# Gate input x^T from plain float32 products in 32x64 array tiles, without block-diagonal halves and stacking DMAs

## The chip, the cores and the metric

The kernel runs on one core of a Trainium2 chip. The metric is the device time of one execution in microseconds (us); less is better. Engines are named as in the profile: PE is the matrix engine, PEld its weight loads, DVE the vector engine, ACT the scalar engine, POOL the general engine, SP the queue that issues the DMAs.

## What is computed

For each of 8 batches, 8 heads, 576 positions and a head width of 64, two attentions run one after the other, then a gated layer, then a spatial gated layer:

```python
p_packed = sm_attn(p, k, v)            # 32 packed queries per head
x = sm_attn(q, p_packed, p_packed)     # 576 x 512 per batch
gate = sigmoid(causal 5-tap convolution of x along the positions, per channel)
y = gate * (x @ w_val) @ w_out
h = relu(y @ w_in); u, v = halves of h
v_n = layer norm of v over its 512 channels
out = (u * (w_spatial @ v_n + b)) @ w_out2
```

The change concerns x, in its transposed form (channels on partitions), that the convolution reads. The product x @ w_val takes another way in both versions (below) and doesn't need x itself.

## The kernel before

Setup turns the weights from float64 words into float32 (`from_f64`: units on ACT, DVE and POOL), multiplies w_out and w_in into one matrix on PE (`fold`), and splits most matrices into a high and a low part in the type float32r. A product of two split matrices is then three float32r products (`mm3`); a plain float32 product needs no split.

The work of one batch is cut into steps with names, and three strings set the order in which they are written: START (setup and the attention of batch 0), FIRST (the rest of batch 0 with the attention of batch 1, mixed with setup) and LOOP (the rest of batch b with the attention of batch b+1). A scheduler then moves instructions within each engine's queue; all queues run strictly in order, and PSUM is a pool `ps2` of four slots of two banks each, so a step that needs a slot waits until the step that had it was copied out. The steps around the change:

- `sa`, `tr`, `av`: scores of p and k, exponentials, product with v. At its end `av` holds in PSUM, for a group g of four heads, 32 rows for each head: the packed values, and their sums in column 64. DVE makes the reciprocal `rs`, ACT writes the scaled values to `pp` (L203). DVE also writes `ppd`, the same values as block-diagonal halves: four multiplications by a 0/1 mask for each group (L199), split into `ppdh` and `ppdl` by `split` (L92 on ACT, L93 on DVE).
- `ppt`, `sb`: `pp` is transposed by PE (L212), copied by ACT (L214), and multiplied with q in plain float32 (L220): 16 products of 64 rows by 32 columns of the array, eight tiles side by side.
- `sb2`: softmax over the 32 packed positions. DVE ends it with `an` (L251), which is split into `Ah` and `Al` for the product with M. Four DMAs for each group (L259, L260) put the halves of `Ah` above those of `Al` in one tile `ad`.
- `m`: M = p_packed @ w_val in plain float32 (L269), eight products of 64x32 tiles and 512 columns, split into `Mh` (ACT) and `Ml` (DVE). x @ w_val is then A @ M, in `val`.
- `xt(g)`: x^T of two heads at a time, so that the channels fill 128 partitions: `ad` times `ppdh`, then `ppdl`, as full 128x128 products in float32r. Two channel tiles c for each g, four products each, 16 for a batch. `conv(c)` follows: ACT copies PSUM to `x` (L288) and writes `acc` with the last tap (L292), DVE adds four taps (L304; in batch 0 some go to POOL), ACT makes the sigmoid `gate` (L308).
- `sp`: the spatial product, 28 products for each of four tiles; DVE multiplies by u out of PSUM (L418), ACT and DVE split the result `g` (L92, L93).
- `out`: the last product, 24 for each of four tiles; `val` of the next round multiplies its result by `gate` on DVE (L331).

Of the kernel before, what the change touches and what calls it, by code (L numbers as in the profile page):

```python
# [18 lines left out]
ADB = 2  # L19
# [3 lines left out]
ik0 ip0 ro0 ic0 ik1 sa0 iv1 uo0 iv0 rw0 tr0 lv0 rv0 ro1 uo1 cw0 rv1 lk0 lq0 rw1 uw0 tr1 uo3 uw1 av0 uw2 uo2 uv0 av1 uv1 uw3 lq1 fv3 fv0 fv1 lk1 ppt0 sb0 sb20 sb21 fv2 xt0 uv3 uv2 lp0 m0 xt1 lv1  # L23
"""
FIRST = """
val1 ru1 val0 val3 ru0 lv0 val2 sa0 uu2 uu0 hv0 uu1 tr0 ws3 tr1 uu3 fu2 fu0 ws4 hv3 wo0 lv1 ws1 hv2 av0 av1 fu1 lq0 fu3 ppt0 lq1 wo1 hv1 hv4 ws0 sb0 hu1 hu2 ws2 sb20 lp0 hu3 sb21 hu0 wo3 lk0 lk1 sp0 sp2 sp1 wo2 sp3 xt0 m0 out1 out3 xt1 out0 out2
"""
LOOP = """
lq0 val1 val0 val2 lp0 val3 hu1 sa0 lq1 hv0 tr0 hv1 hu0 hv4 av0 tr1 av1 hu2 hv2 ppt0 hv3 sb0 sb20 sp1 lv0 sb21 hu3 sp0 sp3 sp2 m0 lk1 xt0 out1 lv1 xt1 out2 out0 lk0 out3
"""  # L30


# [1 line left out]
def packed_attention_gated_mlp(  # L34
# [36 lines left out]
    g_p = ctx.enter_context(tc.tile_pool(name="g", bufs=4))  # L71
    vr_p = ctx.enter_context(tc.tile_pool(name="vr", bufs=2))
    vn_p = ctx.enter_context(tc.tile_pool(name="vn", bufs=1))
    ad_p = ctx.enter_context(tc.tile_pool(name="ad", bufs=ADB))
    ug_p = ctx.enter_context(tc.tile_pool(name="ug", bufs=UGB))
    ps2 = ctx.enter_context(tc.tile_pool(name="ps2", bufs=4, space=bass.MemoryType.PSUM))

# [4 lines left out]
    mask = const.tile([P, 2, 64], F32)  # L82
# [40 lines left out]
    class Attn:  # L123
        def __init__(self, b):
            self.b = b
            self.a, self.aT, self.ppd = {}, {}, {}
            self.sT, self.A = {}, {}
            self.gate, self.ad = {}, {}

        def heads(self, lhsT, kind):  # L130
            src = [kq_t.pop((kind, self.b, i)) for i in range(2)]
# [45 lines left out]
        def av(self, g):  # L177
            aT = self.aT.pop(g)
            v = v_t.pop((self.b, g))
            ps = ps2.tile([P, 2, 512], F32, tag="ps2", name="ps2")[:, 0, :]  # L180
            for t in range(5):
                for h in range(4):
                    nc.tensor.matmul(  # L183
                        ps[NPK * h:NPK * h + NPK, :65],
                        lhsT=aT[:, 9 * (h // 2) + 4 * (h % 2) + t, :],
                        rhs=v[:, h, t, :],
                        start=(t == 0), stop=(t == 4),
                        tile_position=(0, NPK * h),
                    )
# [88 lines left out]
        def xt(self, g):
            ad = self.ad.pop(g)
            for i in range(2):  # L280
                ps = ps2.tile([P, 2, 512], F32, tag="ps2", name="ps2")
                for n in range(2):
# [362 lines left out]
```

## Time and profile before

| what | value |
|---|---|
| median of 3 runs | 643.06 us (642.97 to 643.32) |
| span of the profiled execution, first to last instruction | 642.7 us |
| PE busy | 593.3 us, 92% |
| DVE, ACT, POOL busy | 494.3, 314.7, 88.1 us |
| chain that ended last | PE 83%, DVE 9%, DMA 4%, ACT 2%, issue 2% |
| granted PE clock | mostly full; half in some stretches before 120 us |

No other time of the profiled execution is given than its span; the median lies 0.36 us above it. In the slices of 16 us each the digits are busy shares in tenths; a digit 9 for PE says that it was occupied, not that it ran at its peak, since its products are pipelined and their ends modelled. DMA queue 1 moved 61 MB in 28.8% of the time of its 16 engines.

### The profile page before, as it was taken

The numbers are of one execution on the slowest core, as the hardware profiler recorded it, in microseconds if no ns is written. First come the engines' busy times: TensorE is split into PE (matmuls) and PEld (weight loads), VectorE is DVE, ScalarE is ACT, GpSimd is POOL, SyncE is SP. The second block draws the span as 40 slices with busy tenths as digits, with TensorE's granted clock in tenths as the row PEclk, the third lists the DMA queues.
The fourth block names the chain that finished last, engine by engine and source line by source line (L and its number), as shares of the span: only waits on it lengthen the run. The fifth ranks groups of instructions, "written<-read, shape, count | busy, mean of one in ns | idle before, by whom it ended". The sixth has DMA issues, their size and how long they took to land.

```text
span 642.7 us, 12335 instructions
## 1 busy us (share of the span) xinstructions
PE 593.3 (92%) x5000; PEld 520.1 (81%) x5000; DVE 494.3 (77%) x966; ACT 314.7 (49%) x548; POOL 88.1 (14%) x92
## 2 busy tenths in 40 slices
PE   1466769899999999999999999999999999999997
PEld 0222535699988998899889998899889988999997
DVE  4989988986868877788679876887688867993630
ACT  2635755555554464437443635455444644372412
POOL 2396642221001000100010000100010001000100
PEclk9978789899999999999999999999999999999999
DMA  8961143341133312341323233231243110310001
GB/s 323 409 224 44 31 144 139 108 125 56 58 91 145 74 74 79 120 114 56 97 84 108 59 100 118 76 93 56 74 159 74 75 38 1 75 56 19 1 1 73
DMA packets 21689, 61.91 MB, mean 96 GB/s; under 512 B 2977, under 2 KB 4001, under 8 KB 21634
## 3 DMA queue, kind: packets, MB, share of 16 engines
q1 hardware_dynamic: 21634, 61.14, 28.8%
q8 instruction: 39, 0.64, 0.4%
q14 instruction: 16, 0.13, 0.1%
HBM read 42.25 MB, written 9.44 MB: 80 GB/s over the span
## 4 chain that ended last, share of the span: by engine, by line
PE 83%; DVE 9%; DMA 4%; ACT 2%; issue 2%; SPq 0%; POOL 0%; ACTq 0%; DVEq 0%; POOLq 0%
PE ps L97 77%; DMA stage<-wsT 2%; PE ps L143 2%; DVE acc L304 2%; PE ps L220 2%; PE ps L183 1%; DMA raw<-w_outT 1%; PE ps L269 1%; DVE tmp L460 1%; DVE tmp L464 1%; DVE tmp L459 1%; DVE ppd L199 1%; DMA raw<-w_out 1%; DVE sT L247 0%; DVE sm L245 0%
## 5 line engine op out<-in xcount | busy, mean ns | idle before, releaser
L97 PE MATMUL ps<-ws,vn 128*128 128x288 f32 (+1 forms) x896 | 124.0, 296 | 0.0
L97 PEld LDWEIGHTS ps<-ws,vn 128*128 128x128 f32 (+1 forms) x896 | 120.3, 188 | 2.9 <-issue 2.8
L97 PE MATMUL ps<-g,wp 128*128 128x288 f32 x768 | 114.2, 298 | 0.0
L97 PEld LDWEIGHTS ps<-g,wp 128*128 128x128 f32 x768 | 106.3, 188 | 5.0 <-DVE g L331 1.3
L97 PE MATMUL ps<-g,wo 128*128 128x288 f32 x768 | 104.3, 295 | 0.0
L97 PEld LDWEIGHTS ps<-g,wo 128*128 128x128 f32 x768 | 102.6, 188 | 0.8 <-ACT acc L292 0.8
L97 PE MATMUL ps<-wp,g 128*128 128x512 f32 x384 | 100.1, 411 | 2.9 <-DVE g L331 2.9
L304 DVE SCALAR_TENSOR_TENSOR acc<-x,cw,acc 128x572 f32<-128x572 f32 (+3 forms) x122 | 96.3, 854 | 3.3 <-ACT acc L292 2.8
L97 PEld LDWEIGHTS ps<-wp,g 128*128 128x128 f32 x384 | 72.1, 192 | 22.4 <-issue 3.5
L370 POOL TENSOR_TENSOR rstd<-rstd,mhalf 128x1 f32<-128x1 f32 (+1 forms) x40 | 22.9, 574 | 458.7 <-DVE rstd L369 456.4
L92 ACT CAST g<-g 128x576 fp32r<-128x576 f32 x64 | 43.1, 674 | 85.9 <-DVE g L418 55.0
L93 DVE TENSOR_TENSOR g<-g,g 128x576 fp32r<-128x576 f32 x64 | 48.1, 752 | 9.3 <-ACT g L92 8.9
L397 ACT ACTIVATE u<-ps 128x576 f32<-128x576 f32 x32 | 20.7, 647 | 47.1 <-PE ps L97 47.1
L92 ACT CAST vn<-vr 128x512 fp32r<-128x512 f32 (+1 forms) x40 | 24.7, 619 | 36.2 <-DVE vr L371 36.1
L418 DVE TENSOR_TENSOR g<-ps,u 128x576 f32<-128x576 f32 x32 | 24.1, 754 | 21.0 <-PE ps L97 20.9
L97 PE MATMUL ps<-Ah,Ml 128*128 128x288 f32 x128 | 38.6, 303 | 1.8 <-DVE Ml L93 1.8
L331 DVE TENSOR_TENSOR g<-ps,gate 128x576 f32<-128x576 f32 x32 | 24.1, 756 | 20.1 <-ACT gate L308 13.7
L97 PE MATMUL ps<-Ah,Mh 128*128 128x288 f32 x128 | 38.6, 301 | 0.7 <-ACT acc L292 0.7
L97 PE MATMUL ps<-Al,Mh 128*128 128x288 f32 x128 | 38.5, 301 | 0.0
L365 DVE BATCH_NORM_STATS2 st<-vr 128x6 f32<-128x512 f32 (+1 forms) x40 | 27.3, 683 | 11.8 <-ACT vr L358 10.2
L371 DVE TENSOR_SCALAR vr<-vr,mv,rstd 128x512 f32<-128x512 f32 (+1 forms) x40 | 22.5, 562 | 17.0 <-POOL rstd L370 16.7
L93 DVE TENSOR_TENSOR vn<-vr,vn 128x512 fp32r<-128x512 f32 (+1 forms) x40 | 27.1, 680 | 6.9 <-ACT vn L92 6.8
(115 smaller groups left out, 861.6 us busy)
## 6 DMA issues: line engine op xcount, KB each, us to landing
v<-vT SPq DMA_DIRECT2D x16, 650.0 KB, 5.4
kq<-kT SPq DMA_DIRECT2D x16, 576.0 KB, 4.6
kq<-qT SPq DMA_DIRECT2D x16, 576.0 KB, 4.7
outT<-o SPq DMA_DIRECT2D x32, 288.0 KB, 2.1
ad<-Ah SPq DMA_DIRECT2D x32, 144.0 KB, 2.5
ad<-Al SPq DMA_DIRECT2D x32, 144.0 KB, 2.5
raw<-w_in SPq DMA_DIRECT2D x8, 512.0 KB, 10.2
raw<-w_outT SPq DMA_DIRECT2D x4, 512.0 KB, 8.6
```

What stands on the lines that cost most here:

```text
L92: nc.scalar.copy(out=hi, in_=src)
L93: nc.vector.tensor_tensor(out=lo, in0=src, in1=f32(hi), op=ALU.subtract)
L97: nc.tensor.matmul(out, lhsT=a, rhs=b, start=(i == 0), stop=(i == len(pairs) - 1))
L143: nc.tensor.matmul(ps[g][NPK * qt:NPK * qt + NPK, h // 2, SQ * (h % 2):SQ * (h % 2) + SQ], lhsT=pT_, rhs=k[:, SQ * qt:SQ * qt + SQ], start ...
L220: nc.tensor.matmul(ps[g][NPK * h:NPK * h + NPK, n, :SH], lhsT=pT_, rhs=q[:, n * SH:(n + 1) * SH], start=True, stop=True, tile_position=(64 ...
L304: nc.vector.scalar_tensor_tensor(out=acc[:, sft:], in0=x[:, :S - sft], scalar=cw[:, c, tap:tap + 1], in1=acc[:, sft:], op0=ALU.mult, op1=A ...
L331: nc.vector.tensor_tensor(out=halves(t), in0=ps[:, :, :SH], in1=halves(at.gate.pop(c)), op=ALU.mult)
L365: nc.vector.bn_stats(st[:w], vr[:w])
L370: nc.gpsimd.tensor_tensor(out=rstd[:w], in0=rstd[:w], in1=mhalf[:w], op=ALU.pow)
L371: nc.vector.tensor_scalar(out=vr[:w], in0=vr[:w], scalar1=mv[:w, 0:1], scalar2=rstd[:w], op0=ALU.subtract, op1=ALU.mult,)
L397: nc.scalar.activation(out=halves(u), in_=ps[:, :, :SH], func=AF.Relu)
L418: nc.vector.tensor_tensor(out=halves(t), in0=ps[:, :, :SH], in1=halves(self.u.pop(c)), op=ALU.mult)
```

## The change

x^T is made from `pp` and `an` as they are. Each head is one plain float32 product of 32 rows (its packed positions) by 64 columns (its channels), at array row 32h and column 64g; the heads h and h+4 (g = 0 and 1) lie one above the other in a channel tile. `xt(n)` now makes all four channel tiles for one half n of the positions: 8 products into two PSUM slots, and ACT copies each slot to a half of `x` (a tile with two channel tiles in it). The four convolutions start when both halves are there, and ACT takes the last tap from `x` in SBUF instead of PSUM. `ppd`, its split, the mask and the DMAs to `ad` are gone. The channel order of w_val, conv_w and w_out follows the new pairs, on the host. `an` and `x` get pools of their own. In the strings xt0 and xt1 stand together, in LOOP ahead of m0.

```diff
-lq0 val1 val0 val2 lp0 val3 hu1 sa0 lq1 hv0 tr0 hv1 hu0 hv4 av0 tr1 av1 hu2 hv2 ppt0 hv3 sb0 sb20 sp1 lv0 sb21 hu3 sp0 sp3 sp2 m0 lk1 xt0 out1 lv1 xt1 out2 out0 lk0 out3
+lq0 val1 val0 val2 lp0 val3 hu1 sa0 lq1 hv0 tr0 hv1 hu0 hv4 av0 tr1 av1 hu2 hv2 ppt0 hv3 sb0 sb20 sp1 lv0 sb21 hu3 sp0 sp3 sp2 xt0 xt1 m0 lk1 out1 lv1 out2 out0 lk0 out3
...
-    ad_p = ctx.enter_context(tc.tile_pool(name="ad", bufs=ADB))
+    an_p = ctx.enter_context(tc.tile_pool(name="an", bufs=3))
+    x_p = ctx.enter_context(tc.tile_pool(name="x", bufs=2))
...
-            ppd = pp_p.tile([P, 2, 2, 64], F32, tag="ppd", name="ppd", bufs=1)
-            for i in range(2):
-                r = slice(64 * i, 64 * i + 64)
-                for j in range(2):
-                    nc.vector.scalar_tensor_tensor(
-                        out=ppd[64 * j:64 * j + 64, i], in0=ps[r, :64].unsqueeze(1).to_broadcast([64, 2, 64]),
-                        scalar=rs[r], in1=mask[r], op0=ALU.mult, op1=ALU.mult,
-                    )
             nc.scalar.activation(out=self.pp[:, g, :], in_=ps[:, :64], func=AF.Copy, scale=rs)
...
-            split(hi, lo, ppd)
...
-                nc.sync.dma_start(out=f32(ad)[:64, i], in_=f32(hi)[r])
-                nc.sync.dma_start(out=f32(ad)[64:, i], in_=f32(lo)[r])
...
-                    mms(ps[:, n, :SH], [(w[:, i, :], ad[:, i, n * SH:(n + 1) * SH]) for w in self.ppd[g]])
-                self.conv(2 * g + i, ps)
...
+        def xt(self, n):
+            ss = slice(n * SH, (n + 1) * SH)
+            ps = [ps2.tile([P, 2, 512], F32, tag="ps2", name="ps2") for _ in range(2)]
+            for h in range(4):
+                hs = slice(NPK * h, NPK * h + NPK)
+                for g in range(2):
+                    nc.tensor.matmul(
+                        ps[h // 2][64 * g:64 * g + 64, h % 2, :SH], lhsT=self.pp[hs, g, :],
+                        rhs=self.an[g][hs, ss], start=True, stop=True, tile_position=(NPK * h, 64 * g),
+                    )
+            if n == 0:
+                self.x = [x_p.tile([P, 2, S], F32, tag="x", name="x") for _ in range(2)]
+            for j in range(2):
+                nc.scalar.copy(out=self.x[j][:, :, ss], in_=ps[j][:, :, :SH])
+            if n == 1:
+                for c in range(4):
+                    self.conv(c, self.x[c // 2][:, c % 2, :])
...
-            nc.scalar.activation(
-                out=halves(acc), in_=ps[:, :, :SH], func=AF.Copy, scale=cw[:, c, CONV - 1:CONV]
-            )
+            nc.scalar.activation(out=acc, in_=x, func=AF.Copy, scale=cw[:, c, CONV - 1:CONV])
```

What stands where, in three places. First PE, in a round of LOOP, between the last `sp` product and the first `out`. Names are those of PSUM tiles; a row in square brackets waits for the engine named (the suffix is the same everywhere). Before:

```order
L97 MATMUL ps_3883<-ws_779,vn_739 128x288
L269 MATMUL ps_3917<-wval,ppT 32x512 [waits DVE_49]
L269 MATMUL ps_3917<-wval,ppT 32x512 x7
L97 MATMUL ps_3932<-ad,ppdh 128x288 [waits DMAHW3_49,DMAHW1_49,DVE_49]
L97 MATMUL ps_3932<-ad,ppdl 128x288
L97 MATMUL ps_3932<-ad,ppdh 128x288
L97 MATMUL ps_3932<-ad,ppdl 128x288
L97 MATMUL ps_3947<-ad,ppdh 128x288 [waits DMAHW4_49,DMAHW2_49,DVE_49]
```

Now:

```order
L96 MATMUL ps_3732<-ws_746,vn_706 128x288
L265 MATMUL ps_3766<-an,pp 64x288 [waits DVE_49] x2
L265 MATMUL ps_3766<-an,pp 64x288 x2
L265 MATMUL ps_3767<-an,pp 64x288 [waits DVE_49]
L265 MATMUL ps_3767<-an,pp 64x288 x3
L265 MATMUL ps_3780<-an,pp 64x288 [waits DVE_49]
L265 MATMUL ps_3780<-an,pp 64x288 x3
L265 MATMUL ps_3781<-an,pp 64x288 [waits DVE_49]
L265 MATMUL ps_3781<-an,pp 64x288 x3
L250 MATMUL ps_3824<-wval,ppT 32x512 [waits Activation_49]
L250 MATMUL ps_3824<-wval,ppT 32x512 x7
L96 MATMUL ps_3839<-g,wo_811 128x288 [waits Activation_49]
```

Before, `m` came first and waited for DVE alone, two of the four x^T tiles followed, and the other two stood behind the first `out` tile. Now all 16 x^T products come first, in four PSUM slots, and `m`, which needs one of these four again, waits for ACT. Second, ACT in the same round. Before:

```order
L92 CAST g<-g_3912 128x576
L92 CAST Mh<-ps_3917 128x1024
L288 COPY x<-ps_3932 128x576
L292 ACTIVATE acc<-ps_3932,cw 128x576
L288 COPY x<-ps_3947 128x576
L292 ACTIVATE acc<-ps_3947,cw 128x576
L441 COPY o<-ps_3962 128x576
```

Now:

```order
L91 CAST g<-g_3761 128x576
L272 COPY x<-ps_3766 128x2x288
L272 COPY x<-ps_3767 128x2x288
L272 COPY x<-ps_3780 128x2x288
L281 ACTIVATE acc<-x,cw 128x576 x2
L272 COPY x<-ps_3781 128x2x288
L281 ACTIVATE acc<-x,cw 128x576 x2
L91 CAST Mh<-ps_3824 128x1024
```

The first row of each is the high part of the last `sp` tile's result; behind it `Mh` moved from the first place to the last, and the x copies moved ahead. Third, DVE at the end of `av` in START. Before:

```order
L199 SCALAR_TENSOR_TENSOR ppd<-ps_263,rs,mask 64x128 x4
L460 SCALAR_TENSOR_TENSOR tmp<-raw,tmp 128x512
L193 TENSOR_SCALAR rs<-ps_322 128x1
L464 TENSOR_SCALAR tmp<-tmp 128x512
L93 TENSOR_TENSOR ppdl<-ppd,ppdh 128x256
L194 RECIPROCAL rs<-rs 128x1
L199 SCALAR_TENSOR_TENSOR ppd<-ps_322,rs,mask 64x128 x3
```

Now:

```order
L447 SCALAR_TENSOR_TENSOR tmp<-raw,tmp 128x512
L192 TENSOR_SCALAR rs<-ps_310 128x1
L451 TENSOR_SCALAR tmp<-tmp 128x512
L193 RECIPROCAL rs<-rs 128x1
L454 TENSOR_TENSOR winv<-winv,tmp 128x512
```

The ten `ppd` instructions of the batch are gone, and the setup units (`tmp`, `winv`) close up; the other setup units and the steps of `sb` stand on DVE in nearly the order of before.

## Rows read from the trace of the kernel before

**Rows 1.** Page, parts 1 and 2: busy us by engine; busy tenths in 40 slices.
```profile
PE 593.3 (92%) x5000; PEld 520.1 (81%) x5000; DVE 494.3 (77%) x966; ACT 314.7 (49%) x548; POOL 88.1 (14%) x92
...
PE   1466769899999999999999999999999999999997
...
DVE  4989988986868877788679876887688867993630
```

**Rows 2.** Chain that ended last, from 340 us: start, length (us), what.
```profile
357.17 1.02 PE ps L269 x16
358.19 21.55 PE ps L97 x161
```

**Rows 3.** The same chain, whole execution: the product `sb` and what follows.
```profile
337.77 1.13 PE ps L220 x32
338.90 18.27 PE ps L97 x136
```

**Rows 4.** Timeline, 356.3 to 361.5 us, all engines: start, length, instruction, [idle before].
```profile
357.10 1.09 PE L269 MATMUL ps<-wval,ppT 64*32 64x512 f32 x16
357.21 0.76 DVE L418 TENSOR_TENSOR g<-ps,u 128x576 f32<-128x576 f32 x1 [1.46 <-PE ps L97]
358.00 0.67 ACT L92 CAST g<-g 128x576 fp32r<-128x576 f32 x1 [3.04 <-DVE g L418]
...
358.12 0.40 PE L97 MATMUL ps<-ad,ppdh 128*128 128x288 f32 x1
...
358.36 0.29 PE L97 MATMUL ps<-ad,ppdl 128*128 128x288 f32 x1
...
358.58 1.01 ACT L92 CAST Mh<-ps 128x1024 fp32r<-128x1024 f32 x1
...
359.29 2.41 PE L97 MATMUL ps<-g,wo 128*128 128x288 f32 x17
359.48 0.64 ACT L288 COPY x<-ps 128x576 f32<-128x576 f32 x1
...
360.01 0.75 ACT L292 ACTIVATE acc<-ps,cw 128x576 f32<-128x576 f32 x1
```

**Rows 5.** Timeline of DVE, 348 to 388 us: the convolution's steps of one round.
```profile
360.80 11.85 DVE L304 SCALAR_TENSOR_TENSOR acc<-x,cw,acc 128x572 f32<-128x572 f32 x16
```

**Rows 6.** Waits of PE, whole execution: us in total, times, longest.
```profile
PE ps L220 <- DVE sT L232: 1.0, 1, 1.0
```

**Rows 7.** Timeline of DVE, 20 to 126 us.
```profile
24.10 1.44 DVE L199 SCALAR_TENSOR_TENSOR ppd<-ps,rs,mask 64x128 f32<-64x128 f32 x4
...
32.22 0.42 DVE L93 TENSOR_TENSOR ppdl<-ppd,ppdh 128x256 fp32r<-128x256 f32 x1
...
37.48 0.85 DVE L232 STREAM_TRANSPOSE sT<-ps 128x288 f32<-128x288 f32 x2 [1.96 <-PE ps L220]
...
61.24 0.76 DVE L251 STREAM_TRANSPOSE an<-sT 128x576 f32<-128x576 f32 x1
...
64.96 2.95 DVE L304 SCALAR_TENSOR_TENSOR acc<-x,cw,acc 128x572 f32<-128x572 f32 x2
...
113.99 1.44 DVE L199 SCALAR_TENSOR_TENSOR ppd<-ps,rs,mask 64x128 f32<-64x128 f32 x4
```

**Rows 8.** Timeline of PE, 0 to 130 us, and steady round (chain, from 130 us).
```profile
115.83 0.33 PE L212 MATMUL ps<-ident,pp 128*128 128x128 f32 x1 [2.13 <-ACT pp L203]
...
122.30 1.23 PE L220 MATMUL ps<-kq,ppT 64*32 64x288 f32 x32
...
197.79 2.80 PE ps L97 x12
```

**Rows 9.** Windows: us, PE busy (x), PEld, DVE, ACT, POOL, PEclk, DMA share, GB/s.
```profile
93.60:95.30 1.70, 0.21 (x2) 0.11 (x1) 0.29 (x2) 1.69 (x7) 1.38 (x2) 1.00 0.07 26
113.60:116.00 2.40, 0.27 (x3) 0.17 (x2) 2.31 (x6) 0.54 (x2) 2.32 (x2) 1.00 0.67 213
116.00:120.00 4.00, 4.00 (x13) 3.11 (x13) 3.99 (x8) 3.59 (x9) 0.45 (x1) 0.61 0.01 5
```

More of the change, by code (lines that the diff above doesn't have):

```diff
@@ L18 @@
 UGB = 5
-ADB = 2
 DADD = ('u2', 'o0', 'o1', 'w1', 'w0')
@@ L22 @@
 START = """
-ik0 ip0 ro0 ic0 ik1 sa0 iv1 uo0 iv0 rw0 tr0 lv0 rv0 ro1 uo1 cw0 rv1 lk0 lq0 rw1 uw0 tr1 uo3 uw1 av0 uw2 uo2 uv0 av1 uv1 uw3 lq1 fv3 fv0 fv1 lk1 ppt0 sb0 sb20 sb21 fv2 xt0 uv3 uv2 lp0 m0 xt1 lv1
+ik0 ip0 ro0 ic0 ik1 sa0 iv1 uo0 iv0 rw0 tr0 lv0 rv0 ro1 uo1 cw0 rv1 lk0 lq0 rw1 uw0 tr1 uo3 uw1 av0 uw2 uo2 uv0 av1 uv1 uw3 lq1 fv3 fv0 fv1 lk1 ppt0 sb0 sb20 sb21 fv2 xt0 xt1 uv3 uv2 lp0 m0 lv1
 """
 FIRST = """
-val1 ru1 val0 val3 ru0 lv0 val2 sa0 uu2 uu0 hv0 uu1 tr0 ws3 tr1 uu3 fu2 fu0 ws4 hv3 wo0 lv1 ws1 hv2 av0 av1 fu1 lq0 fu3 ppt0 lq1 wo1 hv1 hv4 ws0 sb0 hu1 hu2 ws2 sb20 lp0 hu3 sb21 hu0 wo3 lk0 lk1 sp0 sp2 sp1 wo2 sp3 xt0 m0 out1 out3 xt1 out0 out2
+val1 ru1 val0 val3 ru0 lv0 val2 sa0 uu2 uu0 hv0 uu1 tr0 ws3 tr1 uu3 fu2 fu0 ws4 hv3 wo0 lv1 ws1 hv2 av0 av1 fu1 lq0 fu3 ppt0 lq1 wo1 hv1 hv4 ws0 sb0 hu1 hu2 ws2 sb20 lp0 hu3 sb21 hu0 wo3 lk0 lk1 sp0 sp2 sp1 wo2 sp3 xt0 xt1 m0 out1 out3 out0 out2
 """
 LOOP = """
-lq0 val1 val0 val2 lp0 val3 hu1 sa0 lq1 hv0 tr0 hv1 hu0 hv4 av0 tr1 av1 hu2 hv2 ppt0 hv3 sb0 sb20 sp1 lv0 sb21 hu3 sp0 sp3 sp2 m0 lk1 xt0 out1 lv1 xt1 out2 out0 lk0 out3
+lq0 val1 val0 val2 lp0 val3 hu1 sa0 lq1 hv0 tr0 hv1 hu0 hv4 av0 tr1 av1 hu2 hv2 ppt0 hv3 sb0 sb20 sp1 lv0 sb21 hu3 sp0 sp3 sp2 xt0 xt1 m0 lk1 out1 lv1 out2 out0 lk0 out3
 """
@@ L81, in packed_attention_gated_mlp @@
     cw = const.tile([P, NC, CONV], F32)
-    mask = const.tile([P, 2, 64], F32)
     ident = const.tile([P, P], F32)
@@ L125, in __init__ @@
             self.b = b
-            self.a, self.aT, self.ppd = {}, {}, {}
-            self.sT, self.A = {}, {}
-            self.gate, self.ad = {}, {}
+            self.a, self.aT = {}, {}
+            self.sT, self.A, self.an = {}, {}, {}
+            self.gate = {}
         def heads(self, lhsT, kind):
@@ L194, in av @@
             nc.vector.reciprocal(rs, rs)
-            ppd = pp_p.tile([P, 2, 2, 64], F32, tag="ppd", name="ppd", bufs=1)
-            for i in range(2):
-                r = slice(64 * i, 64 * i + 64)
-                for j in range(2):
-                    nc.vector.scalar_tensor_tensor(
-                        out=ppd[64 * j:64 * j + 64, i], in0=ps[r, :64].unsqueeze(1).to_broadcast([64, 2, 64]),
-                        scalar=rs[r], in1=mask[r], op0=ALU.mult, op1=ALU.mult,
-                    )
-            nc.scalar.activation(out=self.pp[:, g, :], in_=ps[:, :64], func=AF.Copy, scale=rs)
-            ppd = ppd.rearrange("p a b c -> p a (b c)")
-            hi = pp_p.tile([P, 2, P], F32R, tag="ppdh", name="ppdh")
-            lo = pp_p.tile([P, 2, P], F32R, tag="ppdl", name="ppdl")
-            split(hi, lo, ppd)
-            self.ppd[g] = (hi, lo)
+            nc.scalar.activation(out=self.pp[:, g, :], in_=ps[:, :64], func=AF.Copy, scale=rs)
         def ppt(self, _):
@@ L249, in sb2 @@
             )
-            an = f_p.tile([P, S], F32, tag="f", name="an")
+            an = an_p.tile([P, S], F32, tag="an", name="an")
             nc.vector.transpose(out=an, in_=sT.rearrange("p a b -> p (a b)"))
@@ L255, in sb2 @@
             self.A[g] = (hi, lo)
-            ad = ad_p.tile([P, 2, S], F32R, tag="ad", name="ad")
-            for i in range(2):
-                r = slice(64 * i, 64 * i + 64)
-                nc.sync.dma_start(out=f32(ad)[:64, i], in_=f32(hi)[r])
-                nc.sync.dma_start(out=f32(ad)[64:, i], in_=f32(lo)[r])
-            self.ad[g] = ad
+            self.an[g] = an
         def m(self, _):
@@ L276, in m, with conv @@
             self.M = (hi, lo)
[L278 to L282, printed above, removed]
-                    mms(ps[:, n, :SH], [(w[:, i, :], ad[:, i, n * SH:(n + 1) * SH]) for w in self.ppd[g]])
-                self.conv(2 * g + i, ps)
-        def conv(self, c, ps):
-            x = f_p.tile([P, S], F32, tag="f", name="x")
-            nc.scalar.copy(out=halves(x), in_=ps[:, :, :SH])
+        def xt(self, n):
[15 more added lines that the diff above has]
+                    self.conv(c, self.x[c // 2][:, c % 2, :])
+        def conv(self, c, x):
             gt = ug_p.tile([P, S], F32, tag="ug", name="gate")
@@ L571, in packed_attention_gated_mlp @@
     nc.vector.memset(mhalf, -0.5)
-    nc.vector.memset(mask, 0.0)
-    for h in range(4):
-        nc.vector.memset(mask[32 * h:32 * h + 32, h % 2, :], 1.0)
     t = const.tile([P, NC, DM], F32, tag="ws0", name="woT")
@@ L613, in rows, with by_pair @@
         return np.ascontiguousarray(w.reshape(-1, 128, w.shape[1]).transpose(1, 0, 2))
-    w_val = np.asarray(inputs["moe_w_val"]).reshape(2, 4, D, -1)
+    def by_pair(w, axis):
+        w = np.moveaxis(np.asarray(w), axis, 0)
+        w = w.reshape(2, 4, D, -1).transpose(1, 0, 2, 3).reshape(H * D, -1)
+        return np.moveaxis(w, 0, axis)
     wt, bias = inputs["moe2_w_spatial"].T, inputs["moe2_b_spatial"]
@@ L626 @@
         "pT": pt,
-        "w_val": rows(w_val.transpose(1, 0, 2, 3).reshape(H * D, -1)),
-        "conv_w": rows(np.ascontiguousarray(inputs["moe_conv_w"].T)).reshape(128, -1),
-        "w_outT": rows(np.ascontiguousarray(inputs["moe_w_out"].T)),
+        "w_val": rows(by_pair(by_pair(inputs["moe_w_val"], 0), 1)),
+        "conv_w": rows(by_pair(inputs["moe_conv_w"].T, 0)).reshape(128, -1),
+        "w_outT": rows(by_pair(inputs["moe_w_out"], 0).T),
         "w_in": rows(inputs["moe2_w_in"]),
```

## Prediction

> **What bounds the kernel now.** I read the page first: PE is occupied 92% of the span, and from the eighth slice on its digit is 9 throughout [rows 1]. DVE, with 77%, has 8 or 9 in the second to the eighth. So there are two stages: setup up to about 120 us, and then rounds that are all PE. The chain of waits says the same of a round: every piece of it is PE, one product behind the other [rows 2, 3]. What PE saves in a round comes off the time, and what another engine saves there doesn't. The price of a full float32r product of 288 columns is 18.27 / 136 = 0.134 us [rows 3].
>
> The timeline then shows the place of the change [rows 4]: `m` starts at 357.10, the first x^T product at 358.12, the next one 0.24 later instead of 0.13, and `out` follows at 359.29. With the other eight x^T products, which stand behind the first `out` tile (8 x 0.134 = 1.07), `m` and x^T hold PE for 2.19 + 1.07 = 3.26 us of a round. The reader should also see what DVE and ACT do there: DVE multiplies the last `sp` tile from 357.21 to 357.97, ACT casts it from 358.00, and ACT can start its next instruction at 358.58.
>
> In setup DVE is the busy engine, and the reader is to see where its work and waits lie: `ppd` at 24.10 and 113.99, a wait of 1.96 for `sb` before 37.48 [rows 7], and PE's wait of 2.13 for `pp` before 115.83 [rows 8].
>
> **A round: x^T.** It takes away 16 x 0.134 + 0.11 (the slow first step) = 2.25 us of PE and adds 16 plain float32 products in 32x64 tiles. The trace has no product of that tile. The nearest row is `sb`: the same count, type and columns in 64x32 tiles, also eight side by side, 1.13 us [rows 3]; I take 1.13. Bounds: 1.02, what `m` needs for eight products of 512 columns [rows 2], and 4 x 1.13 = 4.5 if the four row groups don't run side by side. On PE alone this would save 1.1 us in each of the seven rounds with an x^T of the next batch, 7.8 in all.
>
> **A round: the new wait.** I don't count that saving, because of the order that stands above: the 16 products take all four PSUM slots, and `m` needs the first of them again. It waits for ACT's copy of it to `x`, and ACT has the cast of the last `sp` tile ahead of that copy. With the durations of before: the cast starts at 358.00, the copy at 358.58 and, taking 0.64, ends at 359.22 [rows 4]; PE resumes about 0.05 later (pp to L212, [rows 8], came as quickly). So `m` starts at 359.27 instead of 357.10 + 1.13 = 358.23: a wait of 1.04. `m` takes 1.02 and the first `out` product, now the one after a change of tiles, 0.11 more: `out` stands at 360.40 where before it had 359.29 + 1.07 = 360.36, if the other half of x^T is counted in. That is +0.04 a round, and with a slow restart +0.1: **+0.7 us** for seven. Bounds: -1.04 a round if the copy is there in time (-7.3), and +0.5 a round (+3.5) for what is late next.
>
> Late next would be this. `Mh` moved to the end of ACT's list there, so `Ml` on DVE comes behind ten of the convolution's steps. With the copies 0.53 apart (359.48 to 360.01, [rows 4]) the first step starts some 3.9 us after the last `sp` product, the steps are 11.85 / 16 = 0.74 apart [rows 5], and `Ml` ends at about 12.6. The fourth `out` tile needs its slot at 3.3 + 72 x 0.134 = 12.9. A margin of 0.3, and one like it for the copy of the second `out` tile, which stands behind three sigmoids: I count both at nothing, but they are thin.
>
> A rule of the Trainium skill speaks against expecting more here: the page TensorEngine Tiling, section Performance Considerations (PSUM Bottleneck), says that tiling speeds up the engine and not the emptying of PSUM, so the copies may become the bound. By it the 7.8 would be lost as in my working. The trace of before has one sign of it: tiled products waited once for their slot, `sb` for DVE's transposes, 1.0 us [rows 6].
>
> **A round: what costs nothing.** Ten DVE instructions less, two ACT casts less and eight DMAs less for each batch: PE waits for none of them in a round, so they count only in setup. `acc` from SBUF instead of PSUM and the four copies are as many ACT instructions as before; their cover is the 12.9 us of `out` products, and without it each would cost 0.6.
>
> **Setup, up to 87 us.** DVE's `ppd` of batch 0: 8 x 0.36 (1.44 for four) and two splits of about 0.33 (0.42 with its overlap) make 3.5 us [rows 7]. ACT wrote `pp` only behind `ppd`, so `sb` came late and DVE waited 1.96 for it; with `pp` earlier I let that go too: 5.5 at most. What is late next: the first convolution step, which came 3.7 us after the start of the second `an` (61.24 to 64.96, [rows 7]). Now ACT has a cast, three copies, a setup unit and `acc` ahead of it, each 0.5 to 0.65 apart, which is 4.2 to 4.7: up to 1.0 lost. I take 5.5 - 1.0 = **-4.5 us**. The low end is 1.0 (the freed time goes into waiting for weights to land or for POOL), the high end 5.5.
>
> **Setup, 113 to 122 us.** PE's transposition L212 waits 2.13 for `pp`, which stands behind `ppd` (113.99, four of them, end at 115.43). Without `ppd` the reciprocal is done by about 111 and PE, which is there at 113.7, finds `pp` ready: -2.13. Behind that wait the granted clock is 0.61 on average from 116 to 120 [rows 9]. From 115.93 to 122.30 PE does 20 products of 512 columns [rows 8]; in a round 12 of them take 2.80, so 20 would take 4.67: 1.7 lost to the half clock. Together **-3.8 us**; the low end is 0 (something else is waited for), the high end 3.8.
>
> **Sum.** -4.5 - 3.8 + 0.7 = -7.6. The profiled span of 642.7 becomes 635.1, and the median of 643.06, which lies 0.36 above it, becomes 635.5.
>
> **The rivals.**
> - *Little of setup carries.* The setup units wait for weights or POOL instead of `ppd`: 1.0 of the first term and 2.0 of the second: 643.06 - 3.0 + 0.7 = 640.8. For it: DVE, ACT and POOL hand these units to each other, so none is the only bound. Against it: DVE's digits there are 8 and 9 [rows 1], so it is the bound more than the others. 20%.
> - *Setup gives nothing.* Both savings end in a wait that was hidden: 643.06 + 0.7, about 643.5. 8%.
> - *No wait for the copy.* Should ACT reach the copy before PE needs the slot, a round saves 1.1 us: 635.5 - 0.7 - 7.3 = 627.5. Against it is the order on ACT; the cast can't go ahead of the last `sp` product. 5%.
> - *The 32-row tiles overlap badly* (slower). The place is x^T itself, and it decides from 2.2 us on, because until 359.27 the wait covers it. With the row groups one after the other it is 4.5 us, 2.3 more a round: 635.5 + 16 = 651.5. For it: no row has such a tile. Against it: `sb` and `m` overlap all eight of theirs. 7%.
> - *The half clock comes back* (slower). Each new wait of 1.04 drops the clock as the one at 113.7 did: 7 x 1.7 = 12, so 647.5. Against it: at 93.7 PE stood still for about 1.5 us and the granted clock stayed 1.00 [rows 9]. 4%.
>
> **How the numbers follow.** The forecast has 56%, and its own range is 633 to 639 (the new START order on one side, +3.5 in the rounds on the other). The range to hold the time 8 times in 10 reaches from 630 (a part of the round's bound) to 643.5, so that it takes in the two cases of a poor setup; it leaves out the slower ones. A measurement of this kernel can tell 0.2% (1.3 us) from no change. Below 641.8 lie the forecast, the missing wait and most of the first rival, 0.78; within 0.2% the rest of it and the second, 0.11; above, the two slower ones, 0.11.
>
> **What would show it.** In the new profile: x^T (its 32 records, two for each product as in `sb`) in about 1.1 us; ahead of each `m` an idle time of PE of about 1 us, released by ACT's copy to `x`; rounds as long as before, to 0.2 us; no idle time before `ppt` near 110 us, and no half clock behind it; the first round some 8 us earlier than before. I am wrong if the rounds get shorter or longer by more than 0.5 us, if x^T takes over 2.2 us, or if the first `hu` product doesn't move forward.

## The result, and the profile after

The changed kernel took 649.0 us (median of four runs, 648.38 to 649.36), the kernel before 643.19 us beside it: ratio 1.0084, interval 1.0064 to 1.0105. It is slower by 0.8%, where the forecast was 635.5 us with a range that ended at 643.5. One execution of all those behind this document, of the variant mid_both below, took 839.02 us at a mean granted clock of 0.66 instead of 0.96 to 0.98; its median and ratio leave it out.

One number has to be set right first. The profiled execution of the changed kernel has a span of 647.2 us and a time of 649.0, so 1.8 us lie around its span, and each run listed with a span, of either kernel, lies 1.7 to 1.9 above it; the 0.36 us of the prediction was no such distance. The profiled execution of before, with its span of 642.7, was therefore one of some 644.5 us, above its median. The two traces differ by 4.5 us, the medians by 5.8; the traces account for the first number. The second may be somewhat large: beside the variants below, the kernel before had medians of 643.81 to 644.31 us (15 to 23 executions each) instead of 643.19.

Where the 4.5 us arise is read from the starts of the same products on PE (timeline of PE up to 130 us, then the chain of waits):

| station on PE | before | after | difference |
|---|---|---|---|
| x^T of batch 0, from where it runs on | 61.37 | 60.82 | -0.6 |
| first `hv` product of batch 0 | 85.70 | 87.74 | +2.0 |
| fold products behind the exponentials of batch 1 | 95.19 | 99.56 | +4.4 |
| `av` of batch 1 | 105.28 | 112.57 | +7.3 |
| `sb` of batch 1 | 122.30 | 125.70 | +3.4 |
| `sb` of batch 2 | 200.59 | 204.87 | +4.3 |
| `sb` of batch 7 | 543.55 | 548.05 | +4.5 |

So the rounds are as long as before: (548.05 - 204.87) / 5 = 68.64 against 68.59 us. The loss is made in setup, between 61 and 113 us, and part of it is given back up to 126 us.

The page of the changed kernel, its busy time and the slices of PE and its clock, answers to [rows 1]:

```profile
PE 587.7 (91%) x5128; PEld 508.2 (79%) x5128; DVE 470.3 (73%) x881; ACT 309.5 (48%) x532; POOL 86.0 (13%) x92
...
PE   1556378999999999999999999999999999999997
...
PEclk9967597999999999999999999999999999999999
```

PE and DVE both have less to do than before (587.7 and 470.3 us against 593.3 and 494.3), and the kernel is slower: the page's sums don't tell it. The second to sixth slices do, with digits of 5, 5, 6, 3 and 7 for PE where [rows 1] has 4, 6, 6, 7 and 6, and a clock digit of 5 in the fifth.

A round, answering to [rows 4]; timeline of the changed kernel from 361.3 us:

```profile
361.47 1.64 PE L265 MATMUL ps<-an,pp 32*64 32x288 f32 x32
361.58 0.76 DVE L405 TENSOR_TENSOR g<-ps,u 128x576 f32<-128x576 f32 x1 [1.46 <-PE ps L96]
362.37 0.67 ACT L91 CAST g<-g 128x576 fp32r<-128x576 f32 x1 [3.04 <-DVE g L405]
362.39 0.21 PEld L265 LDWEIGHTS ps<-an,pp 32*64 32x64 f32 x8 [0.23 <-DVE g L405]
362.95 1.71 ACT L272 COPY x<-ps 128x576 f32<-128x576 f32 x3
...
363.63 1.09 PE L250 MATMUL ps<-wval,ppT 64*32 64x512 f32 x16 [0.53 <-ACT x L272]
```

`m` waits for the copy of `x`, which stands behind the cast of `g`, as the prediction had it. x^T is longer than assumed (1.64 with a wait of 0.23 for its last slot) and the wait shorter (0.53), so `m` starts 2.16 us after the last `sp` product; the prediction's 1.13 + 1.04 is 2.17. ACT's copy sets that moment, as long as the products are done before it.

What PE waits for in the changed kernel (waits of PE: us in total, times, longest):

```profile
...
PE ps L96 <- ACT Mh L91: 7.5, 1, 7.5
PE ps L265 <- DVE wp L490: 5.9, 2, 5.7
PE ps L96 <- ACT a L164: 5.8, 1, 5.8
...
PE ps L96 <- DVE Ml L92: 4.0, 2, 3.7
PE ps L250 <- ACT x L272: 3.7, 7, 0.5
```

The waits for `Mh` and for the copy of `x` are new; those for the exponentials `a` and for `Ml` were 1.5 and 1.8 us before. Their cause stands on ACT and DVE. Before, `Mh` and `Ml` stood as follows (timeline of all engines, 66 to 73 us):

```profile
66.28 1.03 ACT L92 CAST Mh<-ps 128x1024 fp32r<-128x1024 f32 x1
...
68.17 1.53 DVE L304 SCALAR_TENSOR_TENSOR acc<-x,cw,acc 128x573 f32<-128x573 f32 x2
...
71.23 1.21 DVE L93 TENSOR_TENSOR Ml<-ps,Mh 128x1024 fp32r<-128x1024 f32 x1
```

and in the changed kernel, with the convolution's steps ahead of `Ml` (timeline, 66 to 78 us):

```profile
66.22 0.81 DVE L291 SCALAR_TENSOR_TENSOR acc<-x,cw,acc 128x572 f32<-128x572 f32 x1
...
67.28 9.71 DVE L291 SCALAR_TENSOR_TENSOR acc<-x,cw,acc 128x572 f32<-128x572 f32 x6
...
71.66 0.99 ACT L91 CAST Mh<-ps 128x1024 fp32r<-128x1024 f32 x1
...
76.91 1.21 DVE L92 TENSOR_TENSOR Ml<-ps,Mh 128x1024 fp32r<-128x1024 f32 x1
```

START has `m0` behind both x^T steps now, so `Mh` stands on ACT behind four copies and the convolution's starts (before, behind two), and `Ml` on DVE behind seven convolution steps instead of four, six of them 1.6 us long where a round has 0.74 [rows 5]. Both come 5.4 to 5.7 us later, though `m` itself runs on PE when it did (63.85 us, before 63.89); `val` can't finish without `Ml`, `hv` not without `val`, and on DVE the maxima that the exponentials of batch 1 need stand behind `val`'s results. The chain that ended last goes this way, through `Ml`:

```profile
75.15 1.83 DVE acc L291
76.98 1.14 DVE Ml L92
...
78.17 7.36 PE ps L96 x42
...
99.56 13.08 PE ps L96 x34
```

Then the clock. Windows of PE's standstill and of what followed, changed kernel (columns as in [rows 9]):

```profile
94.00:97.00 3.00, 0.00 (x0) 0.00 (x0) 2.79 (x8) 0.00 (x0) 1.87 (x2) 1.00 0.43 118
97.00:99.50 2.50, 0.00 (x0) 0.00 (x0) 0.00 (x0) 2.47 (x6) 0.00 (x0) 0.83 0.06 25
99.50:101.50 2.00, 1.94 (x3) 0.91 (x4) 1.65 (x3) 2.00 (x7) 0.00 (x0) 0.50 0.07 25
...
103.50:105.50 2.00, 2.00 (x3) 0.67 (x2) 0.32 (x1) 1.67 (x3) 0.56 (x1) 0.50 0.02 6
```

PE stands still for 5.8 us and then works at the lower of its two levels (0.50 of full speed) until 105.5. The 34 products from there to `av` take 112.57 - 99.56 = 13.0 us; before, at the higher level, it was 105.28 - 95.19 = 10.1. That is the step from +4.4 to +7.3.

### The profile page after: what moved, and what is told of

It is laid out like the page before. It is cut to its first block, busy times and chain, and to the rows that moved or that the text cites. A ratio compares the mean times of both kernels' runs of the same rounds, so it can differ in the third digit from the quotient of the medians.

```text
span 647.2 us, 12281 instructions
## 1 busy us (share of the span) xinstructions
PE 587.7 (91%) x5128; PEld 508.2 (79%) x5128; DVE 470.3 (73%) x881; ACT 309.5 (48%) x532; POOL 86.0 (13%) x92
## 4 chain that ended last, share of the span: by engine, by line
PE 82%; DVE 11%; ACT 3%; DMA 2%; issue 1%; POOL 0%; SPq 0%; ACTq 0%; POOLq 0%
PE ps L96 76%; DVE acc L291 3%; PE ps L142 2%; PE ps L182 1%; PE ps L206 1%; DVE tmp L451 1%; DMA raw<-w_outT 1%; DVE tmp L447 1%; ACT x L272 1%; PE ps L250 1%; DVE g L405 1%; ACT g L91 1%; DMA raw<-w_in 1%; DVE tmp L446 1%; DVE m L155 0%
## 5 line engine op out<-in xcount | busy, mean ns | idle before, releaser
L291 DVE SCALAR_TENSOR_TENSOR acc<-x,cw,acc 128x573 f32<-128x573 f32 (+3 forms) x122 | 96.4, 860 | 11.8 <-ACT acc L281 11.7
L96 PE MATMUL ps<-wp,g 128*128 128x512 f32 x384 | 97.0, 402 | 1.0 <-DVE tail L325 1.0
L96 PEld LDWEIGHTS ps<-wp,g 128*128 128x128 f32 x384 | 70.5, 188 | 19.8 <-issue 3.1
L92 DVE TENSOR_TENSOR g<-g,g 128x576 fp32r<-128x576 f32 x64 | 49.1, 768 | 10.5 <-ACT g L91 9.9
L295 ACT ACTIVATE gate<-acc 128x576 f32<-128x576 f32 x32 | 21.9, 686 | 42.7 <-DVE acc L291 40.3
```

The lines of the kernel that those rows point to most:

```text
L291: nc.vector.scalar_tensor_tensor(out=acc[:, sft:], in0=x[:, :S - sft], scalar=cw[:, c, tap:tap + 1], in1=acc[:, sft:], op0=ALU.mult, op1=A ...
L295: nc.scalar.activation(out=gt, in_=acc, func=AF.Sigmoid)
```

## The experiments

My theory after the result (A): `m`'s place in START makes the loss. Its rival (B): the freed DVE time went into waits for weights and POOL, and `m` is no matter. Times are medians, each with its ratio to the kernel before as it ran beside the variant; the ratios are compared, since the median of the kernel before itself shifts by up to 1.1 us.

**start_old.** START as before, in the changed kernel (the end of the string is shown):

```diff
-fv2 xt0 xt1 uv3 uv2 lp0 m0 lv1
+fv2 xt0 uv3 uv2 lp0 m0 xt1 lv1
```

> The changed kernel with the START string of before (xt0, then the setup of w_val, m0, then xt1). Theory A (the place of m in START makes the loss: Mh stands on ACT behind four copies, four acc and the taps, Ml on DVE behind seven convolution steps): Mh and Ml come about 5 us earlier, PE's waits of 7.5 and 3.7 us for them shrink to under 4 in all, the last val product ends near 80 us instead of 85.4, the exponentials of batch 1 start near 95 instead of 99.6, and PE's wait of 5.8 us before them shrinks to 1 to 2 with no half clock behind it (3.0 us). Together 649.0 - 4.4 - 3.0 = about 641.6 us. Theory B (what DVE gained by losing ppd went into waits for the weights and POOL; m's place is no matter): 647.5 to 649.5 us.

647.41 us, ratio 1.0045 (1.0024 to 1.0066): about half the loss is gone. The time alone decides nothing: A had 641.6, and 647.4 lies at the edge of B's range. The timeline of PE shows why:

```profile
81.31 3.13 PE L142 MATMUL ps<-kq,pbd 64*32 64x144 f32 x64 [9.47 <-DVE g L318]
89.32 2.90 PE L96 MATMUL ps<-wp,g 128*128 128x512 f32 x6 [4.88 <-DVE g L318]
...
98.49 4.56 PE L96 MATMUL ps<-winu,woT 128*128 128x512 f32 x10 [0.98 <-ACT a L164]
```

The waits for `Mh` and `Ml` went as A says (0.7 us is left), and `val` is early. But its results need the gates, and now the convolution is late: PE waits 9.5 and 4.9 us for `g`, and the first `hv` comes at 89.32, later than in the changed kernel. The half clock behind the exponentials is gone, as expected; it now lies behind the waits for `g` (0.50 from 84 to 91 us). `sb` of batch 1 stands at 121.94, against 125.70 and, in the kernel before, 122.30. This trace is of the fastest of six executions (645.66 us), so it doesn't hold all of the 0.45% that is left.

**old_m_late.** The kernel before, with the mirror image of that edit (end of the string):

```diff
-fv2 xt0 uv3 uv2 lp0 m0 xt1 lv1
+fv2 xt0 xt1 uv3 uv2 lp0 m0 lv1
```

> The kernel of before with one change: in START, xt1 stands ahead of m0, as in the changed kernel. Theory A: Mh and Ml come late there too; val ends 4 to 6 us later, and the first hu product with it: 647 to 651 us. Theory B (m's place is no matter, the loss is in the new products and copies): 642.5 to 644 us.

651.3 us, ratio 1.0104 (1.0079 to 1.013). The same two waits appear without any of the new products (waits of PE):

```profile
PE ps L97 <- ACT Mh L92: 5.7, 1, 5.7
...
PE ps L97 <- ACT a L165: 4.7, 1, 4.7
```

So this edit of START alone costs 7 us in the old kernel, where B has none. It isn't the mirror image in all: there the second half of x^T waits 3.6 us for the DMAs to `ad` (1.7 before), and `m` behind it starts at 71.18 instead of 63.89, which the changed kernel doesn't have. Together the two runs show that the order in START makes about half of the loss by median, and most of it in the traces. B falls as the main cause.

**chan_start.** As start_old, with x^T cut by channel tiles instead of by halves of the positions (the pool of `x` has four buffers):

```diff
-        def xt(self, n):
+        def xt(self, i):
...
-                        ps[h // 2][64 * g:64 * g + 64, h % 2, :SH], lhsT=self.pp[hs, g, :],
+                            ps[h % 2][64 * g:64 * g + 64, n, :SH], lhsT=self.pp[hs, g, :],
...
+                self.conv(2 * i + j, x)
```

> The run start_old with one more change: xt(i) makes the two channel tiles 2i and 2i+1 for all positions (in the order of the kernel before) instead of all four for half the positions; FIRST and LOOP as in the changed kernel. Theory C (the convolution of all four tiles starts only when both halves of the positions are there; that is why start_old still waits 9.5 and 4.9 us for g at 72 to 89 us): two of the four convolutions start behind xt0, the two waits shrink to about 4 us in all as before, the first hv comes near 86 us instead of 89.3, and the time is about 644 us. Rival D (DVE has the same convolution work either way and is the bound from 64 to 90 us): as start_old, 646.5 to 648.

647.68 us, ratio 1.0059 (1.0042 to 1.0075). Timeline of PE:

```profile
86.94 2.92 PE L96 MATMUL ps<-wp,g 128*128 128x512 f32 x6 [3.38 <-DVE g L316]
...
95.49 2.84 PE L96 MATMUL ps<-winu,woT 128*128 128x512 f32 x6 [0.53 <-ACT a L164]
...
110.02 10.07 PE L96 MATMUL ps<-winu,woT 128*128 128x512 f32 x16 [1.84 <-DVE wp L488]
```

The stations went to where C put them: `hv` at 86.9, the exponentials let PE go on at 95.5, `av` follows at 105.6, nearly the kernel before. The time didn't follow; it is in the range of rival D. In the middle of `av` and behind it PE waits 1.0 and 1.8 us for DVE's copies of the folds, and 16 fold products take 10.07 us instead of 7.13, partly at the half clock (0.50 from 110 to 115 us). C is right about the waits for `g`, and wrong that they set the end of setup.

**dead_ppd.** The changed kernel with `ppd` back as dead work (eight multiplications, two splits and the mask, read by nobody):

> The changed kernel with the work on ppd put back as dead work in every batch: the mask, four multiplications and a split for each group; nobody reads it; pool an has two buffers instead of three to make room. My step on 113 to 122 us (without ppd, pp is ready when PE comes, 2.1 us, and the half clock behind that wait goes, 1.7 us) predicts that both come back: about 652.9 us. My step on the setup up to 87 us (4.5 us) would add 4.5 more: 657. Rival (the loss before it already gave pp time, so that ppd costs nothing now): 648.5 to 650 us.

650.9 us, ratio 1.0094 (1.0074 to 1.0114), which can't be told from the changed kernel's 1.0084; as ratios my two steps together had 1.021, the first alone 1.015, the rival 1.008 to 1.011. The wait for `pp` ahead of its transposition is back with 1.74 us (without a half clock behind it), and from `av` to `sb` of batch 1 it is 126.55 - 111.47 = 15.1 us instead of 13.1. Up to x^T the ten instructions cost next to nothing: from `av` of batch 0 to x^T it is 60.63 - 19.25 = 41.4 us with them, 60.82 - 19.95 = 40.9 without, and 61.37 - 20.51 = 40.9 in the kernel before. What took the place of that work is seen in the windows from 20 to 40 us (columns as in [rows 9]); before:

```profile
20.00:40.00 20.00, 14.01 (x125) 6.26 (x125) 17.33 (x39) 10.13 (x21) 12.44 (x8) 0.91 0.98 370
```

and in the changed kernel:

```profile
20.00:40.00 20.00, 9.99 (x109) 5.11 (x109) 18.16 (x27) 8.90 (x17) 12.83 (x10) 0.93 0.86 325
```

DVE has twelve instructions less and is busy for longer: 18.16 / 27 = 0.67 us each, before 17.33 / 39 = 0.44 (0.47 without the ten of `ppd`, which are short). The timeline of the changed kernel, 33.9 to 36 us, has an instance:

```profile
33.95 1.70 POOL L454 TENSOR_TENSOR winv<-winv,tmp 128x512 f32<-128x512 f32 x1
34.46 1.48 DVE L446 TENSOR_SCALAR tmp<-tmp 128x512 int32<-128x512 int32 x1
```

In the kernel before, steps of that shape took 0.42 us at 32.89 and 34.17. They too lay beside an instruction of POOL, and there it was that one that was long:

```profile
33.12 3.52 POOL L466 TENSOR_TENSOR winv<-winv,tmp 128x512 f32<-128x512 f32 x1 [3.98 <-DVE tmp L464]
...
34.17 0.42 DVE L459 TENSOR_SCALAR tmp<-tmp 128x512 int32<-128x512 int32 x1
```

**loop_mid.** The round, in the changed kernel (a piece of the string is shown):

```diff
-sp3 sp2 xt0 xt1 m0 lk1 out1
+sp3 sp2 xt0 m0 xt1 lk1 out1
```

(and the same in FIRST)

> The changed kernel with m0 between xt0 and xt1 in FIRST and LOOP; START as changed. My reading of the round (m waits for ACT's copy of x because x^T took all four PSUM slots): m finds a free slot, the copies run beside it, and the first out product comes 2.7 us after the last sp product instead of 3.2: seven times -0.5, 645.5 us; no wait of m for the copy of x left. Rival (Ml is now ahead of the convolution on DVE, and the late gates make val wait by as much): 648.5 to 649.5 us, with a new wait of PE for g.

645.75 us, ratio 1.0029 (1.0012 to 1.0045). Round of (543.45 - 202.20) / 5 = 68.25 us; timeline:

```profile
358.03 0.74 PE L265 MATMUL ps<-an,pp 32*64 32x288 f32 x16
...
358.70 1.09 PE L250 MATMUL ps<-wval,ppT 64*32 64x512 f32 x16
...
359.72 1.19 PE L265 MATMUL ps<-an,pp 32*64 32x288 f32 x16
360.19 0.21 PEld L265 LDWEIGHTS ps<-an,pp 32*64 32x64 f32 x8 [0.27 <-ACT x L272]
360.84 1.35 PEld L96 LDWEIGHTS ps<-g,wo 128*128 128x128 f32 x10 [0.44 <-ACT x L272]
```

`out` starts 2.81 us after the last `sp` product, where I had 2.7. The wait for the slot is confirmed as the thing that ate the products' gain, and eight products that run freely take 0.67 us.

**chan_all and all_old.** The old strings throughout, with x^T by channel tiles and by halves.

> x^T by channel tiles as in chan_start, and all three strings as in the kernel before, so that the plain products, the missing ppd and the missing DMAs are what is left of the change. My price for x^T (16 products at about 0.6 to 0.7 us for eight, against 2.25 before) then shows in each round: period 68.59 - 0.9 = 67.7 us, seven times, and with chan_start's setup 636 to 638 us. Rival (with two channel tiles at a time only four tiles of the array run side by side, so eight products cost 1.1 us and not 0.6): rounds as before, 642 to 643.5 us.

> The changed kernel with its x^T by halves of the positions, but all three strings as in the kernel before: the second half comes behind the first out tile. Theory C: the convolution starts 3.3 us later in each round, the last gates come late, and PE waits for g before the next scores or hu; what the products save is lost there, 647 to 654 us. Rival (the 12.9 us of out products cover it): period 67.7 and 641 us.

chan_all took 648.71 us (ratio 1.0075, 1.005 to 1.01), with a round of (546.76 - 202.12) / 5 = 68.93; all_old 649.5 us (1.0085, 1.0055 to 1.0115), with 68.68. In the first the rival holds for the products, as the chain of waits says:

```profile
360.40 1.13 PE ps L266 x16
```

With two row groups of the array at a time four tiles work, not eight, and eight products take 1.13 us: no gain over the old 1.07. Its time is above both forecasts, with rounds 0.3 us longer than before; where that lies was not traced. In the second the products are quick, but PE waits for the exponentials, 1.9 us in setup and 0.5 to 0.7 in each of six rounds. By the order on DVE the late second half and the late gates would be the reason; no run tried it. Most of its loss lies ahead of the rounds: `sb` of batch 2 stands at 206.31, before at 200.59, with waits of 7.9 and 4.9 us for `g`.

**fill.** The changed kernel with 24 products of a zero matrix in PE's standstill:

```diff
...
+                fill = [(zero, w_hi[0])] * (24 if (self.b, tt) == (0, 0) else 0)
...
```

> The changed kernel with 24 products of a zero matrix added to the first hv tile of batch 0, which the order puts into PE's wait for the exponentials (5.8 us from 93.7 to 99.6); they add zeros. Theory (the half clock from 99 to 105.5 us comes from PE's standing still, and costs 3.0 us): the granted clock stays 1.00 there, av of batch 1 comes 3 us earlier, 646.0 us. Rival (the clock falls for another reason, or the fill only delays): 649 us or more.

651.72 us, ratio 1.012 (1.0086 to 1.0155). The window in which PE stood still and the clock fell in the changed kernel, now:

```profile
97.00:99.50 2.50, 2.50 (x9) 1.51 (x8) 0.85 (x2) 2.49 (x10) 0.00 (x0) 1.00 0.07 26
```

and the timeline of PE:

```profile
97.94 4.45 PE L97 MATMUL ps<-winu,woT 128*128 128x512 f32 x10
...
108.42 0.78 PE L183 MATMUL ps<-v,aT 128*32 128x65 f32 x40
113.63 1.31 PE L183 MATMUL ps<-v,aT 128*32 128x65 f32 x40 [4.43 <-DVE wp L493]
```

With PE kept at work the clock stays full, and `av` comes at 108.42 instead of 112.57 (of these 4.2 us, 1.3 are there at the first `hv` already, 86.48 against 87.74; the 34 products take 10.5 us instead of 13.0): without the standstill there is no half clock. But the gain is not kept. The second half of `av` waits 4.4 us for DVE's copy of a fold, and behind that wait the clock is lower again (0.74 on average from 114 to 122 us). The time as a whole is the rival's.

**old_pp.** My third term by itself, in the kernel before: `pp` is written ahead of the `ppd` multiplications, which stay.

```diff
+            nc.scalar.activation(out=self.pp[:, g, :], in_=ps[:, :64], func=AF.Copy, scale=rs)
             ppd = pp_p.tile([P, 2, 2, 64], F32, tag="ppd", name="ppd", bufs=1)
...
-            nc.scalar.activation(out=self.pp[:, g, :], in_=ps[:, :64], func=AF.Copy, scale=rs)
```

> The kernel of before with one line moved: pp is written ahead of the four ppd multiplications, which stay. My term on 113 to 122 us by itself (PE's wait of 2.13 us for pp, and the half clock behind it, 1.7 us): 3.8 us less, ratio 0.994; with the wait gone and the half clock not, or elsewhere, 0.997. Rival (the wait is only handed on, to sb's transposes or to DVE's backlog): 0.999 to 1.001.

644.86 us, ratio 1.0011 (0.9998 to 1.0024). Timeline of PE:

```profile
108.03 0.78 PE L183 MATMUL ps<-v,aT 128*32 128x65 f32 x40 [2.44 <-DVE wp L503]
110.69 8.52 PE L97 MATMUL ps<-winu,woT 128*128 128x512 f32 x16 [1.87 <-DVE wp L503]
119.05 0.27 PE L212 MATMUL ps<-ident,pp 128*128 128x128 f32 x1
```

The wait of L212 for `pp` is gone, and two others, for DVE's copies of the folds, have taken its place; the rival holds.

**mid_both and mid_chan0.** Both repairs of the order together (start_old and loop_mid), and the same with x^T by channel tiles in batch 0 alone.

> The changed kernel with both repairs of the order: START as before (as in start_old) and m0 between xt0 and xt1 in FIRST and LOOP (as in loop_mid). If the two are independent, as I read them (setup and round), the times add: against the kernel before, start_old's 1.0045 and loop_mid's seven rounds at 68.25 instead of 68.64 (-2.7 us, -0.0042): ratio 1.000, within 0.002, 643 to 645 us. Rival (the setup of start_old is late in DVE work that the shorter rounds then wait for): 1.004 as start_old.

> As mid_both, but for batch 0 alone x^T is made by channel tiles as in chan_start, so that two convolutions start behind xt0 there; the other batches make it by halves, eight tiles side by side. Expected: the waits for g of 9.5 and 4.9 us go as in chan_start, the scores' exponentials of batch 1 come near 95.5 us. If what chan_start lost afterwards (folds that wait for DVE, 2.9 us, and a half clock on 16 fold products, 2.9 us) was particular to that run, 640 to 642 us; if DVE's backlog is the bound up to 125 us whichever way PE is ordered, as mid_both, 643 to 645.

mid_both took 644.45 us (ratio 0.9999, 0.9988 to 1.001) and mid_chan0 644.14 us (1.0002, 0.9988 to 1.0015). The two repairs add up as expected, and the time is that of the kernel before again. That doesn't mean that setup is as fast as before: start_old alone keeps 0.45%, and the rounds, 68.25 us against 68.59, win it back. Cutting batch 0 the other way changes nothing: in that run PE waits 1.6 and 1.8 us for the folds' copies again, as in chan_start.

**mid_dve.** mid_both, with the first copy of `x` on DVE from batch 1 on:

```diff
-                nc.scalar.copy(out=self.x[j][:, :, ss], in_=ps[j][:, :, :SH])
+                copy = nc.vector.tensor_copy if self.b and (n, j) == (0, 0) else nc.scalar.copy
+                copy(out=self.x[j][:, :, ss], in_=ps[j][:, :, :SH])
```

> As mid_both, but from batch 1 on DVE makes the first of the four copies of x, which on ACT stands behind the cast of the last g. In loop_mid's round the second half of x^T waited 0.27 us for that copy and the first out product 0.44 for the next one. If both come 0.2 to 0.3 earlier, the round is 68.0 instead of 68.25 us, seven times: ratio to the kernel before 0.997. Rival (the low part of the last g, now behind the copy on DVE, comes 0.7 us late and out waits for it): 1.000 or above.

641.93 us, ratio 0.9962 (0.9944 to 0.9979): faster than both kernels. Chain of waits:

```profile
355.94 0.67 PE ps L265 x16
356.61 1.02 PE ps L250 x16
357.63 0.67 PE ps L265 x16
```

PE waits for nothing at this place any more; the round takes (539.96 - 200.93) / 5 = 67.81 us.

## Why the prediction was wrong, step by step

**A round: the sum and the mechanism were right.** Predicted was +0.04 a round, at most +0.1; measured is +0.04. The wait for ACT's copy, which stands behind the cast of `g`, is there in all seven rounds, and loop_mid and mid_dve show that it held back the gain. Two parts were off against each other: sixteen products take 1.34 us when nothing stops them (2 x 0.67), not the 1.13 of `sb`, and the wait was 0.53, not 1.04. That the sum held is no luck, since ACT's copy ends when the prediction said and is the last to end. The first round lost 0.9 instead of 0.1; 0.3 of it is the wait for `Ml` at the fourth `out` tile, whose margin I had called thin, and 0.3 is `sb` of batch 1 itself (1.42 us in the chain, before 1.16). The rest was not found.

**Setup up to 87 us: this step failed.** It had -4.5 us; the first `hv` came 2.0 us later and the exponentials 4.4. It went wrong in two places.
- I followed the move of `Mh` and `Ml` in a round, where `out` covers it, and not in START, where nothing does. There I named the first convolution step as what is late next. The order of both queues could have told it before any run: `Mh` behind four copies, `Ml` behind seven steps. old_m_late shows the price, 7 us in the kernel before (with a longer wait for the DMAs to `ad` in it), and start_old gives about half of the loss back in the changed one.
- I took the freed DVE time as time gained. x^T of batch 0 came 0.6 us earlier, but so did `av` of batch 0 (19.95 against 20.51), ahead of the first removed `ppd` instruction: between the two nothing was gained (40.9 us both times), and dead_ppd puts the work back for 0.5 us. The place of the removed instructions went to setup units, and DVE's instructions became longer (0.67 us each instead of 0.44). In the rows the long ones lie beside POOL's work on the same weights; so do short ones of the kernel before, where POOL's was long. That the two engines hold each other up was not tried.

**Behind the exponentials: a step that was missing.** The rival with the half clock had it in the rounds, from a wait of about 1 us; there no clock fell. It fell in setup, behind a standstill of 5.8 us, and cost 2.9 us on the way to `av` (2.5 by fill, which keeps it up).

**113 to 122 us: the size was right, the worth was not.** From `av` to `sb` of batch 1 it is 125.70 - 112.57 = 13.1 us, before 122.30 - 105.28 = 17.0: -3.9 where I had -3.8, with no wait ahead of `ppt` (L198) and no half clock behind it. The agreement is in part luck: dead_ppd has the work and the wait back and loses 2.0 of the 3.9, but has no half clock, so that the other 1.9 can't be put down to `ppd`. And old_pp takes the same wait out of the old kernel and gains nothing. The wait was one of several ends of the same backlog on DVE and ACT. In five runs (chan_start, chan_all, fill, old_pp, mid_chan0) PE came to `av` earlier than in the changed kernel and then waited for DVE's copies of the folds instead.

**The rivals.** By its number the half clock's 647.5 us came nearest, by luck, since no wait in a round dropped the clock. "Setup gives nothing" is nearest in what it says of setup, but its mechanism (savings that end in hidden waits) has no way to lose 4 us, and of the two slower rivals neither named the place. The tiles don't overlap badly, unless only half of them are used: eight products with four tiles side by side take 1.13 us, with eight 0.67. What I lacked was a rival in which a step that the change moves in START comes late.

**What stays open.** What bounds the stretch from `av` to `sb` of batch 1 once PE gets there early: the chain of mid_chan0 has DMAs of later weights there and ACT's units behind them, but no run took these away. What keeps start_old 0.45% slower is open too: its late gates are one candidate, but chan_start has them earlier and is no faster. POOL's part in DVE's long instructions is not shown. And 1.3 us of the 5.8 lie between the profiled execution of before and its median, not in either trace's rows.

The rule on tiling that the prediction set beside its row (the Trainium skill, TensorEngine Tiling, section Performance Considerations, PSUM Bottleneck) agrees with the runs: the quick products were worth nothing until the copies kept up. The same section advises to empty PSUM with ACT and DVE both; mid_dve does that, and its round is 68.25 - 67.81 = 0.44 us shorter.

## What to carry to other kernels

When a change rewrites an order, follow each moved step through every stage that uses it. A step whose lateness is covered in the steady rounds can stand on the critical path during setup, where it is paid only once but in full. Work taken off a busy engine need not be time gained: here the next units took its place and ran longer. And a faster product is worth what its PSUM slots allow, so place another step between its halves and let two engines copy.

## What was not expected of the hardware

- Plain float32 products of 32x64 tiles and 288 columns: eight took 0.67 us with eight tiles in use and 1.13 us with four. The second is no quicker than eight full float32r products (1.07).
- PE's clock fell to the lower level behind a standstill of 5.8 us and stayed there for about 6 us of work; with products of zeros in that standstill it stayed at the higher one.
- DVE steps of one shape took 0.42 us in one run and 1.48 us in another at nearly the same time, both beside instructions of POOL; where DVE's were short, POOL's took 3.52 us, and where they were long, 1.70. The Trainium skill (Advanced Engine Details and Errata, section VectorE Performance Modes, Mode Summary) says that DVE's second port to SBUF is shared with POOL, and that POOL's instructions and those of DVE that use both ports block each other. The rows fit that; no run here separates the two.
